# Another fixed order for an attention and expert kernel: 64-row matmul steps in longer runs

## The chip, the core and the metric

The kernel runs on one core of a Trainium2 chip. The metric is the device time of one execution in microseconds. Before the change it is 367.17 us, the median of three runs (366.87 to 367.61). A profiled execution spans 365.3 us; the profile's views count from the start of that span. The core's engines are PE (matmuls, with PEld for loading their weights), DVE (vector), ACT (scalar functions), POOL (GpSimd) and SP, which here only issues transfers. Each engine works through its own instructions in the order in which the program gives them, and waits where it needs another engine's result or a buffer that is still in use.

## What is computed

A linear attention with an exponential feature map, for 8 x 8 heads of 576 tokens and 64 dimensions, and then a two-layer network with an ELU between, for all 4608 tokens:

```python
def phi(x):
    proj = np.einsum('bhsd,df->bhsf', x, w_phi)               # 64 -> 128 features
    proj = proj - np.max(np.abs(proj), axis=-1, keepdims=True)
    return np.concatenate([np.exp(proj), np.exp(-proj)], axis=-1)
q_p, k_p = (phi(q), phi(k))
kv = np.einsum('bhsf,bhsd->bhfd', k_p, v)
z = np.sum(k_p, axis=2)
num = np.einsum('bhsf,bhfd->bhsd', q_p, kv)
den = np.einsum('bhsf,bhf->bhs', q_p, z)[..., None] + 1e-06
x = (num / den)                                               # then heads side by side: 4608 x 512
h = x @ w_in                                                  # 512 -> 2048
g = np.where(h > 0.0, h, np.exp(np.minimum(h, 0.0)) - 1.0)
out = g @ w_out                                               # 2048 -> 512
```

## The kernel before

The 64 heads are worked on in 16 groups of four, and the 4608 tokens of the network in 9 chunks of 512. The program is a list of small steps, each a Python function that emits a few instructions. A string fixes their order: one letter for each step, a star for a variant on another engine or with another layout, and a digit for the first PSUM bank that a PE step writes. The n-th occurrence of a letter is the n-th piece of that kind of work. There are 8 banks; steps A, M, S, U and W take two neighbouring ones, the others one.

```python
ORDER = """
eacdbeefgj7kfA0gj7BekBA2A4fCBj7hl6Bkl1hmBmA6gCBM0BCj3DBkENA4Dl3BEOmBP2l1EQCS2m*CFA0FTM6ECU4DTUNE
...                                     # 30 lines in all
"""
    STEPS = dict(
        ...
        e=(load, ...k...), f=(load, ...q...), g=(load, ...v...),       # POOL issues the loads
        h=(load_w_in, PAIR), i=(load_w_out, [()]),
        j=(t_pe, ...), k=(t_copy, ...), l=(t_pe, ...), m=(t_copy, ...), # k and q of groups 0-3, transposed on PE
        n=(t_dma, [("k", n) for n in range(PT, NG)]),                   # groups 4-15: transposed by DMA, issued by SP
        o=(t_dma, [("q", n) for n in range(PT, NG)]),
        A=(k_mm, ...), B=(k_exp, ...), C=(k_max, ...),                  # k's projection, two exponentials, maximum
        D=(v_exp, ...), E=(v_scale, ...), F=(v_ones, ...),              # v scaled by exp(-max), on POOL
        M=(m_mm, ...), N=(m_max, ...), O=(m_split, ...), P=(m_pe, ...), Q=(m_copy, ...),   # q's maximum
        S=(q_mm, ...), T=(q_exp, ...),                                  # q's projection, exponentials
        U=(kv_mm, ...), V=(kv_copy, ...),                               # kv and z
        W=(x_mm, ...), X=(x_div, ...), x=(x_join, ...), R=(x_rec, ...), y=(x_scale, ...),  # num, den, division
        Y=(x_pe, ...), Z=(x_copy, ...), z=(x_dma, ...),                 # the result transposed
        p=(h_mm, chunk_parts), q=(h_exp, chunk_parts), r=(h_min, chunk_parts), s=(h_elu, chunk_parts),
        t=(o_mm, ...), u=(o_copy, o_tiles), v=(o_store, o_tiles),
    )
    for letter, star, bank in re.findall(r"([A-Za-z])(\*?)(\d?)", "".join(ORDER.split())):
        ...
        fn(*next(args), **how)
```

The steps that the prediction speaks of. The head dimension is 64, so k's and q's projections contract over 64 rows only, and two heads sit above each other in a tile; kv contracts over 64 tokens. These matmuls use half of PE's rows each ("64*128" in the profile); all other steps use the whole array ("128*128").

```python
def k_mm(n, c, bank=None, other=False):                      # A: 6 matmuls, 64 rows
    ...
    for i3 in range(3):
        for par in range(2):
            rows = slice(par * D, (par + 1) * D)
            nc.tensor.matmul(pj[:, par, i3, :], st["kT", n][rows, 3 * c + i3, :], w_sb[rows, :],
                             start=True, stop=True)

def k_exp(n, c, sg):                                         # B, twice on each A's banks: ACT
    nc.scalar.activation(EK[...], st["pk", n, c], ACT.Exp, scale=1.0 - 2.0 * sg)

def k_max(n, c):                                             # C, on the same banks: DVE
    nc.vector.tensor_reduce(mk[...], st["pk", n, c], axis=AX.X, op=ALU.max, apply_absolute_value=True)

def kv_mm(n, pr, bank=None):                                 # U: 36 matmuls, 64 rows
    ...
                    rows = slice(hi * D, (hi + 1) * D)
                    nc.tensor.matmul(kv[:, hi, pr, sg, :], EK[rows, sg, pr * NS + s, :],
                                     vs[rows, sg, pr * NS + s, :], start=(s == 0), stop=(s == NS - 1))

def t_dma(name, n):                                          # n, o: from group 6 on q goes in two halves
    nat = st[name, n // 2][:, 2 * (n % 2):2 * (n % 2) + 2]
    out_t = get((name + "T", n), new_t(name))                # tpool has bufs=2: two kT, two qT
    if name == "q" and n >= JOINED:
        ...
        for hi in range(2):
            nc.sync.dma_start_transpose(out=out_t[:, hi], in_=nat[hi * D:(hi + 1) * D]...)
        return
    ...

def h_mm(ch, jt, h0, h1, bank=None):                         # p: 4 matmuls of 512 columns (chunk 0: 256)
    ...
def h_exp(ch, jt, h0, h1): nc.scalar.activation(e_sb, st["ph", ch, jt, h0], ACT.Exp)      # q: ACT
def h_min(ch, jt, h0, h1): nc.gpsimd.tensor_scalar(e_sb, e_sb, 1.0, 0.0, ...)            # r: POOL
def h_elu(ch, jt, h0, h1): nc.vector.scalar_tensor_tensor(gT[:, jt, h0:h1], e, -1.0, ph, ...)  # s: DVE

def o_mm(ch, tt, part, bank=None):                           # t: 4 matmuls of 512 columns
    ...
```

M works like A on q (the maximum of q's projection has rows and features the other way round than S), S projects q with 64 rows and 384 columns at a time, and W multiplies with all 128 rows. A bank is free for the next PE step when its readers are done: B, B and C for A; T, T for S; N for M; q, r and s for p; u for the last t of an output tile.

Of the kernel before, what the change touches and what calls it, by code (L numbers as in the profile page):

```python
# [15 lines left out]


ORDER = """
eacdbeefgj7kfA0gj7BekBA2A4fCBj7hl6Bkl1hmBmA6gCBM0BCj3DBkENA4Dl3BEOmBP2l1EQCS2m*CFA0FTM6ECU4DTUNE
BM2EOVDBNFW6EP5M0XM2Q*S4ENTU6FNOj1iP0UQ*kTS2VM0TNW4TY7OXS0j6Tl3kTY2mP5l4Z*W0mQ*Z*S3XA5Tp7j2qkTS0  # L20
rCp2TM3TsNqp7BrA0sj4qCp3Brp2qsl6BkresM4qmp7BrNp3qM0qsrA4Drsp6Esp2qNl7Bp3rqp1O*sqrY0mrCZ*W6FEsp0B
XP2gqp5Drp4qQqsrS6srqM2sFTsEM0NTp5rNqp7rS2qsM0sTrY6ENU4TsA0O*A2BUZp7VBp6qP5CBt4rsBS0p7TCtqQ*rW2T
sp5DnXqW0qrtrXfp6ES2qsA0stBnrFsTp7Eu*t6TCp5qp4rDzqp3sqrp2Brszp7sqp5qrqS0rstrTsoFsEqp4Tp7rqzS2sA0
rTtEsCToU4qA2BUrzstV*CBW4up7XW0qBt6rXzDBM4FtNzM0M2sA4NvBp7tNqBzrA0sM2O*BCftBENP7t5uQCEDS2M6TtNFe
TS0M6ETtNTEU2S0A6UTCop4VtqTp3rzBsW0qnp4Xrp2qszW0rqu*O*p3DXvBEp5qsvrp7qrszp6rqsFsA0rqM2np4NBEp5qC
rzP3p2rQ*sqp3srqsDp7rqsfp6sqrBp5rsqEsM0qA2p4NBrt7BrsqFS0CgtTsrTS2EM5TNS0toTsTA5U2CTUBS0VvtBW2zTt
6XTW4uzA0DXS2BtETzCtFETtzBA2M4BS0t7oTCtDTNFtEBvM0A4EM2NBtzNeBU0fu*UA2Cp6Bp5Cqut4rDBsEp7qM2V*rp6N
qEDnW0wstwrqxgM2trNW0FnetxEp5vusS0qM2Rp7syTNp6TFrqS2Rp4qsrTrsp5qsTp7rqysW0qS2xp6rTzrTp4sEzsqA0U2
qCroUrsBp7RV*syA5BCW2p4zxDqW0Eqxp3Brp2rBsRqA0S5qCnt7rTgRtsvTrstBEvsDS3M5TytNzTt2yu*BW3EzS5xA0tBF
zTRM3CtyTNFtzBEwM5S0vU3NTUToA5Vt7BuA0CtCzDtBEW2BtfxBA4p6BRyp3CqDEW0u*wp2qxrBp7FqFsrS0M4TEt6NTtrs  # L30
qtRrsM0ysM3p5NEzp7qNp2rzqsW0rqp4nxrp5qevstrsqsrS0uU2RTUy*S6TzVp4TsW0vqp3xTrp5qoRrsA0qS6p2CTrp4Ts
vqsW6qp3rzBrsp5qexBt2rqRS0DA6srotBsytBsyTA3CtETCzW5Dt7FxFBEtBnRM0yA5M3NBztEutNBzEM0wU2CvfUNDS4V*
Et6uW0TvW2xTtxA4M0BntRBW2Nyzp7ECtqt1xFDrup5FsEA2qM6p4NBrp0ECqU6srBUqM2V*tNrA5sS2Bp7swRp4TRCyqp0T
rztqsBtzrqgy*S2u*W5Torp7xDTp1sqS2qRvW5rsTp4rsTp0zyxqW2Fqp7zrsrsA5qvp1gRBxrp4qsBp3rsqyp2Cqrwzt7sq
rsS0EM5sTtnNTrtEDzsS0M3A5TEtCoTt2NFBEA0U3BCURM5Dty*BEVztBNEW3zu*A0S5xBtTt7CTW3RDtxBEA5wM0Bu*FS3y
tNBEtTCp2TFuW0qU3xM5rURM0NV*p7yNp4zqsrS5qA0p3sTroCp2Tqsp7qrW4qrsp6DrsBnp3Rqsp2qrvxBt7rzqsA0S4srB
tsBp6y*TCzp3qRp2qrvwtrsqzsDtrTEsvM0A3M5NBp2ENp1qBru*p0qEsvt7qCFrM5p2rsW3NqtrstFsExA0S5BtyTCt4TRW
2By*txzDA0U5BRS2zUyBtEV*zCtuFDEvW0TS5xt7TEzTtu*ETS0U2TFS4UwTtVW0p6xp3qRTRW0rtqyTp2rxp5qsp4rqRW0r
sqp6sursp3yqsp7qrzxp5rqy*zp4qrssW0rzqt6Rrsp3zxp7qy*W0rsqp2xrp5qstrsqtRrsp4systqzRp7rzst5qtrvsty*
tzt7ztvttt4ttp3p2qp1rqstrqsp3rsp2qt1rqsp0rsp3qtrqsp2rsp0qu*p3rqvstrqsup6rvsp5qp3rqsp2rqsp6rqstrq  # L40
st5rsp3p6qp2rqstrqsp3rsp6qutrqvsp7rsp3qp6rqstrqsup7rvst4qutrvstup7vp6qtrqst5rsp7u*p6qvtrqstrstt7
p6p4qtrqsp3rstqtrsp6t4qutruvstvtt7utvttt6tutvtt7u*tvttuv
"""


# [769 lines left out]
```

## Time and profile before

| | |
|---|---|
| time, median of 3 runs | 367.17 us |
| span of the profiled execution | 365.3 us |
| granted PE clock | 1.00 in every window, 0.96 in the last (340 us to the end) |
| busy: PE, DVE, ACT, POOL | 347.5, 269.6, 251.8, 213.2 us |
| first matmul | at 4.6 us |
| loads of k, q, v, each batch | 576 KB, landing 7.3 to 9.2 us after their issue (medians) |
| loads of w_in (two), w_out | landing 20.4 us after their issue (medians) |
| tiling changes between PE steps | 160 |

The page's second part cuts the span into 40 slices of 9.1 us and gives each engine's busy share in tenths. Its fourth part follows the chain of waits back from the last instruction. Other views are used below: windows (busy time of each engine in chosen stretches), instructions in order of time (start, length, engine, line, operation, output and inputs, how many), and the source view of one line (how often, how long, from issue to landing for transfers). A line such as L693 is that of the printed kernel: L287 is A, L298 B, L305 C, L346 and L361 M, L469 and L481 S, L509 U, L542 and L558 W, L665 p, L676 q, L681 r, L685 s, L693 t. Matmul ends are modelled in the profile and overlap, so the spacing of starts says what a step costs, not the length of its bar.

### The profile page before, as it was taken

To read this page: it belongs to the slowest core of one execution; us is meant where nothing else is said; L and a number is where in the kernel's file an instruction comes from. 1 tells how busy PE (TensorE), PEld (TensorE's weight loads), DVE (VectorE), ACT (ScalarE), POOL (GpSimd) and SP (SyncE) were. 2 spreads that over 40 slices of the span, in tenths; PEclk is the share of its full clock that TensorE was granted. 3 is DMA by queue.
4 is the path that set the end of the run, shared out by engine and by line. 5 is a ranking of instruction groups with operands and counts; after the bars stand their busy time and mean duration, and the time that the engine had idled before them with its cause. 6 is when DMAs were issued, how large, how long until landed. Compare 5 with 4: busy or idle time off the path is not lost.

```text
span 365.3 us, 9809 instructions
## 1 busy us (share of the span) xinstructions
PE 347.5 (95%) x3914; PEld 188.5 (52%) x3914; DVE 269.6 (74%) x476; ACT 251.8 (69%) x479; POOL 213.2 (58%) x323
## 2 busy tenths in 40 slices
PE   3788899999999999999999999999999999999994
PEld 2566676655465454545455445544555444444442
DVE  4899986878876889798978899899858814744300
ACT  4879788877897689877976886888577304554220
POOL 8673848277934988485776597556557404543200
PEclk9999999999999999999999999999999999999999
DMA  7999969599796999866989399053220330214143
GB/s 106 195 213 208 208 100 148 65 166 151 114 144 95 166 171 144 152 89 92 193 162 126 44 173 135 4 110 79 44 48 16 32 75 2 58 29 92 26 99 74
DMA packets 68478, 39.70 MB, mean 109 GB/s; under 512 B 48336, under 2 KB 62800, under 8 KB 68432
## 3 DMA queue, kind: packets, MB, share of 16 engines
q1 hardware_dynamic: 52416, 20.56, 33.1%
q0 software_dynamic: 15856, 18.35, 32.7%
q8 instruction: 30, 0.49, 0.6%
q14 instruction: 16, 0.13, 0.1%
q10 hardware_dynamic: 160, 0.16, 0.1%
HBM read 36.77 MB, written 9.44 MB: 126 GB/s over the span
## 4 chain that ended last, share of the span: by engine, by line
PE 77%; DVE 12%; DMA 7%; issue 1%; POOL 1%; ACT 0%; DVEq 0%; ACTq 0%; POOLq 0%
PE banks L693 32%; PE banks L665 29%; PE banks L509 4%; DMA kT<-kn 3%; DVE mk L305 3%; PE banks L542 3%; PE banks L469 2%; PE banks L287 2%; DVE gT L685 2%; DMA kn<-in_k_dram 2%; DMA qn<-in_q_dram 2%; PE banks L558 2%; DVE mq L388 2%; PE banks L346 2%; DVE xp L575 1%
## 5 line engine op out<-in xcount | busy, mean ns | idle before, releaser
L681 POOL TENSOR_SCALAR e_sb<-e_sb 128x512 f32<-128x512 f32 (+1 forms) x160 | 91.1, 574 | 96.2 <-ACT e_sb L676 93.1
L693 PE MATMUL banks<-w_out_sb,gT 128*128 128x512 bf16 x576 | 138.3, 380 | 0.0
L676 ACT ACTIVATE e_sb<-banks 128x512 f32<-128x512 f32 (+1 forms) x160 | 88.1, 561 | 62.1 <-PE banks L665 57.9
L685 DVE SCALAR_TENSOR_TENSOR gT<-e_sb,banks 128x512 bf16<-128x512 f32 (+1 forms) x160 | 97.0, 626 | 44.9 <-POOL e_sb L681 44.5
L665 PE MATMUL banks<-xT,w_in_sb 128*128 128x512 bf16 (+1 forms) x576 | 123.0, 356 | 1.1 <-DVE gT L685 0.3
L665 PEld LDWEIGHTS <-w_in_sb 128*128 128x128 bf16 x640 | 59.1, 98 | 58.9 <-issue 2.6
L298 ACT ACTIVATE EK<-banks 128x768 bf16<-128x768 f32 x96 | 75.7, 814 | 16.5 <-PE banks L287 14.5
L324 POOL TENSOR_TENSOR vs<-vn,em 128x576 bf16<-128x576 bf16 x64 | 73.6, 1159 | 17.8 <-ACT em L315 17.7
L693 PEld LDWEIGHTS <-gT 128*128 128x128 bf16 x576 | 52.3, 98 | 59.7 <-issue 1.9
L493 ACT ACTIVATE Eq<-banks 128x768 bf16<-128x768 f32 (+2 forms) x96 | 73.5, 813 | 6.9 <-PE banks L481 3.3
L305 DVE TENSOR_REDUCE mk<-banks 128x6 f32<-128x768 f32 x48 | 45.2, 950 | 6.2 <-ACT EK L298 3.9
L374 DVE TENSOR_REDUCE mx<-banks 128x6 f32<-128x768 f32 (+1 forms) x30 | 30.7, 1038 | 4.8 <-PE banks L346 3.8
L608 POOL TENSOR_TENSOR xj<-xs,recj 128x448 bf16<-128x448 f32 (+1 forms) x22 | 20.1, 916 | 13.9 <-DVE recj L603 10.6
L587 DVE TENSOR_TENSOR xs<-banks,e 128x455 f32<-128x455 f32 (+1 forms) x30 | 18.0, 602 | 7.4 <-PE banks L542 5.9
L703 ACT COPY o_sb<-banks 128x512 f32<-128x512 f32 x23 | 13.3, 589 | 14.5 <-PE banks L693 14.5
L509 PE MATMUL banks<-vs,EK 64*128 64x65 bf16 x1152 | 22.9, 192 | 0.2 <-DVE xp L575 0.2
L509 PEld LDWEIGHTS <-EK 64*128 64x128 bf16 x1152 | 20.9, 96 | 2.9 <-issue 1.3
L542 PEld LDWEIGHTS <-Eq 128*128 128x128 bf16 x400 | 16.2, 97 | 7.3 <-issue 1.3
L592 DVE TENSOR_TENSOR xs<-banks,xs 128x455 f32<-128x455 f32 (+1 forms) x30 | 18.3, 610 | 1.1
L287 PE MATMUL banks<-w_sb,kT 64*128 64x128 bf16 x288 | 17.1, 228 | 1.9 <-DVE kT L240 1.1
L542 PE MATMUL banks<-kv_sb,Eq 128*128 128x65 bf16 x400 | 17.2, 193 | 0.5 <-DVE kv_sb L519 0.5
L469 PE MATMUL banks<-qT,w_sb 64*128 64x384 bf16 (+2 forms) x102 | 16.4, 324 | 0.5 <-DVE gT L685 0.2
(66 smaller groups left out, 243.3 us busy)
## 6 DMA issues: line engine op xcount, KB each, us to landing
out_dram<-o_sb SPq DMA_DIRECT2D x71, 128.0 KB, 2.4
kn<-in_k_dram POOLq DMA_DIRECT2D x7, 576.0 KB, 9.2
qn<-in_q_dram POOLq DMA_DIRECT2D x7, 576.0 KB, 7.3
vn<-in_v_dram POOLq DMA_DIRECT2D x7, 576.0 KB, 8.6
w_in_sb<-in_moe_w_in_dram POOLq DMA_DIRECT2D x2, 1024.0 KB, 20.4
w_out_sb<-in_moe_w_out_dram POOLq DMA_DIRECT2D x1, 2048.0 KB, 20.4
qn<-in_q_dram POOLq DMA_DIRECT2D x2, 288.0 KB, 7.4
vn<-in_v_dram POOLq DMA_DIRECT2D x2, 288.0 KB, 8.1
```

The source lines that it names most:

```text
L298: nc.scalar.activation(EK[:, sg, 6 * c:6 * c + 6, :].rearrange("p (i r) f -> p r i f", r=2), st["pk", n, c], ACT.Exp, scale=1.0 - 2.0 * sg,)
L305: nc.vector.tensor_reduce(mk[:, 6 * c:6 * c + 6].rearrange("p (i r) -> p r i", r=2), st["pk", n, c], axis=AX.X, op=ALU.max, apply_absolute ...
L324: nc.gpsimd.tensor_tensor(get(("vs", n), new_vs)[:, sg, r, 0:D], st["v", n // 2][:, 2 * (n % 2) + pr], st["em", n][:, sg, r].unsqueeze(2). ...
L374: nc.vector.tensor_reduce(mq.rearrange("p (v r) -> p r v", r=2)[:, :, v0:v1], st["pm", n, c][:, :, 0:v1 - v0, :], axis=AX.X, op=ALU.max, a ...
L493: nc.scalar.activation(Eq[:, sg, :, :, p0 * D:p1 * D].rearrange("p h r x -> p r h x"), st["pq", n, c][:, :, 0:(p1 - p0) * P].rearrange("p ...
L509: nc.tensor.matmul(kv[:, hi, pr, sg, :], EK[rows, sg, pr * NS + s, :], vs[rows, sg, pr * NS + s, :], start=(s == 0), stop=(s == NS - 1),)
L542: nc.tensor.matmul(pn[:, sg, v - v0, :], Eq[:, sg, hi, par, i0 * D:(i0 + 2) * D], kv_sb[:, hi, pr, sg, :], start=True, stop=True,)
L665: nc.tensor.matmul(ph, w_in_sb[:, ct, jt * P:(jt + 1) * P], xT_of(ch)[:, ct, h0:h1], start=(ct == 0), stop=(ct == N_CT - 1),)
L676: nc.scalar.activation(e_sb, st["ph", ch, jt, h0], ACT.Exp)
L681: nc.gpsimd.tensor_scalar(e_sb, e_sb, 1.0, 0.0, op0=ALU.min, op1=ALU.max)
L685: nc.vector.scalar_tensor_tensor(gT[:, jt, h0:h1], st["e", ch, jt, h0], -1.0, st["ph", ch, jt, h0], op0=ALU.add, op1=ALU.max,)
L693: nc.tensor.matmul(po, st["gT", ch][:, jt, tt * P:(tt + 1) * P], w_out_sb[:, jt, :], start=(jt == 0), stop=(jt == N_JT - 1),)
```

## The change

Only the order string is replaced. The steps are the same ones, 1797 of them, 550 on PE, with the same stars; what differs is their order on each engine's queue and the banks that PE steps write. The new string lets steps with 64-row matmuls stand together in longer runs, so that PE goes from 64-row to 128-row tiling or back 128 times and not 160. The place of a letter in the string orders it only against steps on the same engine; against other engines it is ordered by the data and buffers that they share.

```diff
@@ -16,30 +16,30 @@
 ORDER = """
-eacdbeefgj7kfA0gj7BekBA2A4fCBj7hl6Bkl1hmBmA6gCBM0BCj3DBkENA4Dl3BEOmBP2l1EQCS2m*CFA0FTM6ECU4DTUNE
-BM2EOVDBNFW6EP5M0XM2Q*S4ENTU6FNOj1iP0UQ*kTS2VM0TNW4TY7OXS0j6Tl3kTY2mP5l4Z*W0mQ*Z*S3XA5Tp7j2qkTS0
-rCp2TM3TsNqp7BrA0sj4qCp3Brp2qsl6BkresM4qmp7BrNp3qM0qsrA4Drsp6Esp2qNl7Bp3rqp1O*sqrY0mrCZ*W6FEsp0B
-XP2gqp5Drp4qQqsrS6srqM2sFTsEM0NTp5rNqp7rS2qsM0sTrY6ENU4TsA0O*A2BUZp7VBp6qP5CBt4rsBS0p7TCtqQ*rW2T
-sp5DnXqW0qrtrXfp6ES2qsA0stBnrFsTp7Eu*t6TCp5qp4rDzqp3sqrp2Brszp7sqp5qrqS0rstrTsoFsEqp4Tp7rqzS2sA0
-rTtEsCToU4qA2BUrzstV*CBW4up7XW0qBt6rXzDBM4FtNzM0M2sA4NvBp7tNqBzrA0sM2O*BCftBENP7t5uQCEDS2M6TtNFe
-TS0M6ETtNTEU2S0A6UTCop4VtqTp3rzBsW0qnp4Xrp2qszW0rqu*O*p3DXvBEp5qsvrp7qrszp6rqsFsA0rqM2np4NBEp5qC
-rzP3p2rQ*sqp3srqsDp7rqsfp6sqrBp5rsqEsM0qA2p4NBrt7BrsqFS0CgtTsrTS2EM5TNS0toTsTA5U2CTUBS0VvtBW2zTt
-6XTW4uzA0DXS2BtETzCtFETtzBA2M4BS0t7oTCtDTNFtEBvM0A4EM2NBtzNeBU0fu*UA2Cp6Bp5Cqut4rDBsEp7qM2V*rp6N
[... the other 21 lines of the old order are cut; the printed kernel has them ...]
+eeacdj2j5kbA0kA3BBBA6CCDBBej1j5kkA1BBBCCfgl0ml3mA4M6A2BBCDDNOfl0ml1m*gCP4M6NBBM0QS2efTTM4FEEhOFE
+EFENNU6UVM0P4Q*OP5Q*DS6M2NNW0XS4Tj3j2TTTj7kA0BBkkA2BCECEhEU4FUS0l7l6VW4mmTTgY1BZ*W6XXiOP0Q*DY5Z*
+S2TTM0NM4Np6qrp7qrFessS2TTl1mp0qA5BBCM3Np7qrp2qp1qrrp6sssrsY4p0p5p2p3qqqO*qrsrsrsrsW6XZ*p1p2p0A4
+qrsqrqrsDFqrBp6qssj3P1QY7BECZkp2S0S4rsqrsTTTl3mM6M0TS2TM4NNNEU6TEEUVA0CA2CBBBp4p5p6W0XzqqO*rsDEr
+sfBqrst7tW1Xttu*P0p6p4qrsqrp3qp5p7p2p6qDrrssqrqQ*ssrqp1qrrp3p7qssqrrsp2qssrsS5S0EEfETTTt3tp2tp7T
+FS0qrsqrTtusTU4FUV*gnA2BBA6BBCCDFeEt0W4tW2ozXXtM6NM4NtuM2NO*A6BBt1nA4BCCBDtzzoM2P7QtS4TNM6Nvtu*
+M2NEEEFfS6TTTU4S0UTTzzA2VzCp6W4Xzovp1p7qDrsqqBBrsW4XO*rsp0qrsp6qA2BCp1p5p4qBp7p3P0qqErsqrsDqQ*nn
+A1rrrFsssBBM5Np4p0p7rsCqErqqrsrp5p6qqrsssM3NS0TzzzTt2p5rsqS0S3oTTTTM6NtrsttS4uM6NgFEEgvvTTU0UVS2
+TTA6BBCDEEt4W0XW2XzzzztA0BBA5CCBBttu*t7S2ToDTA0CBBM5tttM2NNwDA4CBBeFnfeU0EEFUM2Np6V*W4p0W1p3xEEq
[... the other 21 lines of the new order are cut ...]
-p6p4qtrqsp3rstqtrsp6t4qutruvstvtt7utvttt6tutvtt7u*tvttuv
+sp0p7p3p5vruvqqruvssrsqqrsrt1ttstut2tttut5tttt1tttvu*vvuv
 """
```

Of the new order, line 3 holds the first p (`Np6q`), and line 8 the last q projection of group 5 and the first maximum projection of group 7 (`S3oTTTTM6NtrsttS4uM6`).

More of the change, by code (lines that the diff above doesn't have):

```diff
@@ L24 @@
-rTtEsCToU4qA2BUrzstV*CBW4up7XW0qBt6rXzDBM4FtNzM0M2sA4NvBp7tNqBzrA0sM2O*BCftBENP7t5uQCEDS2M6TtNFe
-TS0M6ETtNTEU2S0A6UTCop4VtqTp3rzBsW0qnp4Xrp2qszW0rqu*O*p3DXvBEp5qsvrp7qrszp6rqsFsA0rqM2np4NBEp5qC
-rzP3p2rQ*sqp3srqsDp7rqsfp6sqrBp5rsqEsM0qA2p4NBrt7BrsqFS0CgtTsrTS2EM5TNS0toTsTA5U2CTUBS0VvtBW2zTt
-6XTW4uzA0DXS2BtETzCtFETtzBA2M4BS0t7oTCtDTNFtEBvM0A4EM2NBtzNeBU0fu*UA2Cp6Bp5Cqut4rDBsEp7qM2V*rp6N
-qEDnW0wstwrqxgM2trNW0FnetxEp5vusS0qM2Rp7syTNp6TFrqS2Rp4qsrTrsp5qsTp7rqysW0qS2xp6rTzrTp4sEzsqA0U2
-qCroUrsBp7RV*syA5BCW2p4zxDqW0Eqxp3Brp2rBsRqA0S5qCnt7rTgRtsvTrstBEvsDS3M5TytNzTt2yu*BW3EzS5xA0tBF
@@ L30 @@
[L30 to L41, printed above, removed]
@@ new lines @@
+FS0qrsqrTtusTU4FUV*gnA2BBA6BBCCDFeEt0W4tW2ozXXtM6NM4NtuM2NO*A6BBt1nA4BCCBDtzzoM2P7QtS4TNM6Nvtu*
+M2NEEEFfS6TTTU4S0UTTzzA2VzCp6W4Xzovp1p7qDrsqqBBrsW4XO*rsp0qrsp6qA2BCp1p5p4qBp7p3P0qqErsqrsDqQ*nn
+A1rrrFsssBBM5Np4p0p7rsCqErqqrsrp5p6qqrsssM3NS0TzzzTt2p5rsqS0S3oTTTTM6NtrsttS4uM6NgFEEgvvTTU0UVS2
+TTA6BBCDEEt4W0XW2XzzzztA0BBA5CCBBttu*t7S2ToDTA0CBBM5tttM2NNwDA4CBBeFnfeU0EEFUM2Np6V*W4p0W1p3xEEq
+DuqxrsrsEp4p5p1p0qqrrRssqqqrt3FFrrsRssS4TTS6TTtW1yyxRtp0EvneqrM6M4S1oTTvzzNNwwtuyp7qrssp6qrA0A3B
+CCBp5p2p7U0UgqrssBBqrV*A3CBvnvzzsp6qqrrW0xp5t2BssW3xqrsDDS0TTp7qRFERtS0TTrsEM3A5BCBttNyW0xt7tS5T
@@ new lines @@
+TA3BBCDM0Nttu*uM5NEyEU0FUVA6BBERyCDEA4CEES2TBTBt0tW6xttW1W5zzRu*vzzvzxRyxop4qFrsp3p1p2p5p0wqqrsr
+FqrqqM3ssNrsS6TTt1tM6NA4M2NCRynzy*rsBBvttuzzDp3S4TqoU6UVS1TTTp0qrsW6W4xxp3p2p1qp4p7p6rsqqqFrErrs
+srssp0p5qqA1znrsrRsqqEfrrBBCDEyRyS3TTt7sstttS3oM0NM5Nt2tTTwvuvA0BA3CW6xttBBBA6BFCCEezDFEU0UV*M3N
+t5BW0REuDyEEFA3BBCxS6zzzTTtttuW0S6TTRxRM3Nt2tA0CS5ovTTBBtW3yxtu*vvp5qryRy*M6M3NNsU0UV*p2wwW0xRp7
+p5p6p0qrsqp1qDrrqqrgsqfW2ssxp4qp7p6qrrssrrS2A0RqryysssTTp5p4W2xBBCp6qqqp7qrrssrp2qrrp1qsssrsS4TT
+FDFt0tnnA6CBBS4TTM2Nzzzzozzttt7A5BA1BBBRy*zCM3NttS3TTM5EEEEDgEu*CDEENtu*U0UVS5TTA3CBBt2W0xtRW5xt
@@ new lines @@
+tuA3BBM5NCM0p7p2p6qrp4qqqNRrrsS0TTDwssrsp3qp7p6yyrqrqrsW0p4qt2trsssEp7tqxFFA0CU5M3UNRBBtvu*S0V*T
+TW5rW3xy*xp2qp0wqsRFrsp1p5p6rsqqqrrrp7qrssssp2qrsnoA0CA3Ct5BtBBBtDtvuA6BCM1NW3zyxt5ttDDBS1S3M6NT
+TTTtt0EEEFEM1NU6UV*S3TTtEEFFEW6W1ttvzzu*Ry*ERyxxU5UVS3S1TTwTTvuzzt7tW5W3tRRzzzp2p1p0qqqzyyzzxRxv
+vvW4y*rsxrsp3qtp5p4qqp2rsqrsp0p3p1rrrqRRy*sqsu*W4xt6p7p5qsqrsqtrrp2sqzzyvzzRy*zrrssp0p3p4rqrssqs
+rsqrstp7tut5tttp3qrqp2qrrp0p1sssqqrsp4up7p3p0p2qqp6rrrsssqrqqqrrrsssp5qsrsp7t3tttqrut6p3qrp5p0tt
+tqrqrvut1tsssszp2qp7qttt3vuttp0tt4trsrqrvvvu*p5p6sp3ttt2p1tttqqrrqsqrrsssp5p7p3qrssqrqp1p6qqsrsr
```

## The prediction

> **What bounds the kernel now.** I read the slices of the page first, then the chain that ended last, then the windows, then the instructions in order of time.
>
> ```profile
> PE 347.5 (95%) x3914; PEld 188.5 (52%) x3914; DVE 269.6 (74%) x476; ACT 251.8 (69%) x479; POOL 213.2 (58%) x323
> PE   3788899999999999999999999999999999999994
> DVE  4899986878876889798978899899858814744300
> PE 77%; DVE 12%; DMA 7%; issue 1%; POOL 1%; ACT 0%; DVEq 0%; ACTq 0%; POOLq 0%
> 0.00:10.00 10.00, 3.41 (x32) 2.04 (x32) 4.47 (x10) 4.79 (x7) 8.52 (x17) 1.00 0.77 109
> 30.00:40.00 10.00, 8.98 (x114) 7.02 (x113) 9.92 (x21) 8.99 (x22) 5.61 (x12) 1.00 1.23 208
> 60.00:80.00 20.00, 20.00 (x336) 12.04 (x334) 14.98 (x28) 16.66 (x33) 12.44 (x21) 1.00 0.76 117
> ```
>
> A window row gives length, then the busy time of PE, PEld, DVE, ACT, POOL. Up to about 45 us PE has gaps and DVE is the full engine (9.92 of 10 us from 30 to 40); after that PE is busy in every slice until the last store. So two stretches with two bounds: DVE and the loads at the start, PE afterwards. A time saved on PE counts fully only in the second.
>
> Busy does not mean useful, so I split PE's time further. The spacing from one step's first matmul to the next step's shows what a step really costs:
>
> ```profile
> 149.85 0.34 PE L346 MATMUL banks<-w_sb,qT 64*128 64x128 bf16 x6
> 150.02 0.33 PE L469 MATMUL banks<-qT,w_sb 64*128 64x384 bf16 x2
> ...
> 152.57 0.34 PE L287 MATMUL banks<-w_sb,kT 64*128 64x128 bf16 x6
> 152.84 1.90 PE L693 MATMUL banks<-w_out_sb,gT 128*128 128x512 bf16 x8
> 154.58 0.60 PE L542 MATMUL banks<-kv_sb,Eq 128*128 128x65 bf16 x14
> 155.02 1.03 PE L693 MATMUL banks<-w_out_sb,gT 128*128 128x512 bf16 x4
> 155.98 0.34 PE L287 MATMUL banks<-w_sb,kT 64*128 64x128 bf16 x6
> ```
>
> The first column is the start. Six 64-row matmuls followed by another 64-row step take 150.02 - 149.85 = 0.17 us; the same six followed by a 128-row step take 152.84 - 152.57 = 0.27. Eight 512-column matmuls followed by a 128-row step take 1.74 (0.87 for four); four followed by a 64-row step take 155.98 - 155.02 = 0.96. Each change of tiling, in either direction, costs about 0.10 us. Over all steps of this trace the medians are 0.863 without and 0.959 with a change for four 512-column matmuls, 0.178 and 0.274 for six 64-row ones: **0.096 us a change**.
>
> With such undisturbed spacings for every kind of step, PE's time is: steps 321.8, 160 changes x 0.096 = 15.4, waits 19.0, before the first matmul 4.6, after the last 4.6; together 365.4, the span but for rounding. Of the 19.0 of waits 15.4 lie before 60 us. After 60 us there are only 3.6 in 300 us, so in that stretch the changes are paid in full.
>
> **What the Trainium skill says.** "TensorEngine Tiling (Array Packing)", section Key Properties: changing the tiling mode, not just the tile, drains TensorE. It gives no figure; this trace agrees and gives 0.096 us. "TensorE: Matmul & The Clock Gate", section Back-to-back issue gap: columns / 2.4 + 2.5 ns, which is 216 ns for 512 columns; the trace has 863 / 4 = 216, so PE already runs at that pace and only changes and waits are left to save. "PSUM — Partial Sum Buffer", section on bank collisions: two engines must not use one bank at once, reads included. The trace agrees: DVE's absolute maximum waits for ACT's exponential on the same bank (3.9 us in 6 waits). So a bank with k's projection is held for two exponentials and one maximum, one after another.
>
> **The change, part by part.** Counting letters, both orders have the same 1797 steps, 550 of them on PE, with the same number of starred variants; no engine gets more or less work.
>
> (1) Tiling changes. Walking over the PE letters (A, M, S, U without a star are 64-row, all others 128-row) I count 160 changes before and 128 after: 32 x 0.096 = **3.1 us less on PE**. Not all of it can count: up to the 16th input-layer step (p) there were 30 changes and there are now 22. Those 8 lie where PE waits for DVE, so 8 x 0.096 = 0.8 us buys nothing there. Left: **-2.3 us**.
>
> (2) The start. I add up DVE's work (start-to-start: maximum 0.865, 256-column ELU 0.33, division 1.19 us and so on) from the first maximum to a step that frees a bank PE needs, and subtract the PE work that the order puts between. The largest excess is 8.9 us before and 10.2 after: up to there more DVE work stands ahead of the same PE work. Against this, all of k's first two groups now come ahead of q's, which fills DVE while q still loads: in the old run it idled about 1.9 us between 8.9 and 11.2 us. The order of the first 13 loads on POOL's queue is unchanged; w_in's now stand behind scaling steps, but by my reckoning are still issued before the queue reaches them (old landings 26.4 and 31.4 us). I call the start **even, plus or minus 1.5 us**, beyond the 0.8 already taken off.
>
> (3) A transposed tile's buffer. qT has two buffers, so group 7's transposes cannot start until the last q projection of group 5 has read its own. In the old order at least 9.0 us of PE work stood between that and group 7's first use (the maximum projection M). In the new one I find S3 (group 5) M6 t t t S4 M6 (group 7): 0.18 + 3 x 0.863 + 0.17 and two changes = **3.1 us**. Group 8 has 4.7. The source view of the transposes says how long they need:
>
> ```profile
> L254 SPq DMA_TRANSPOSE qT<-qn x20: 1201/1275/2309, 80.2 to 240.4; - x20
> ...
> DMA to landing us min/median/max: 2.9/4.7/6.3
> ```
>
> One head's landing takes 4.7 us from issue and M of group 7 reads only the first head, so it should wait 4.7 - 3.1 = **1.6 us**; if it must wait for both heads, 1.3 more. Group 8 stands behind another transpose on the same queue and should wait about 0.7. Sum **+2.3 us**.
>
> (4) Other banks. For every PE step I compared the PE work since its bank was last filled with what the readers need (two exponentials and a maximum 2.6 us, exponential, minimum and ELU 2.3). Old: 3 places short, by 0.15 us in all. New: 8 places, by 2.1 in all, mostly behind k's projections. Several of them hide behind one another or behind the wait of (3); I take **+0.5**.
>
> (5) Old waits that may not come back. The old steady stretch had single waits of 0.63 (at 225 us), 0.31 (142) and 0.25 (133); the last two follow a late k tile, which the chain of waits shows from 122 to 134 us. The new order has other gaps there; I take **-0.8**.
>
> Sum: -2.3 + 0 + 2.3 + 0.5 - 0.8 = **-0.3 us**, so 366.9 us.
>
> **Rivals.** A: the drains are all that matters and the new order's waits are as small as the old ones. For it: ACT's and DVE's running sums stay within 0.3 us of PE's in both orders nearly everywhere after the start, so the new order seems built with the same care. Then 367.2 - 3.1 = about 364, or 364.9 with the start's 0.8. B: transposes and loads take the place of the drains. For it: the 3.1 us between S of group 5 and M of group 7, the landings of up to 6.3 us, and chunks 1, 3, 4 and 7, whose transposed input has a margin of 0 to 1 us by my sums, against 3 to 6 before. If M waits for both heads in both groups and two chunks start late, +3 to +4 us on mine: about 370. C: the start stays DVE-bound longer. For it the 10.2 against 8.9; then +1.3, about 368. Against a large loss from C: between the 24th and the 32nd input step the new order has 6.8 us of PE work beside only about 4 of DVE, so DVE catches up there.
>
> **Range and chances.** Rival A's 364 and B's 370 are the ends that I can name; a little outside them I put 363.3 to 370.6. A gain of over 2% needs 359.8 us, more than all 32 changes can give together with the steady waits' 3.6; a loss of over 2% needs 374.5, twice what B costs.
>
> **What would show each step.** Four 512-column matmuls at 0.86 and 0.96 us again, and 128 changes: (1). DVE idle between 8 and 12 us gone, and the accumulated PE wait at about 50 us within 1.5 of the old 20: (2). PE idle of 1 to 3 us at L346, released by the DMA of qT, at about 100 to 120 us: (3); if it is absent, the framework's buffers turn faster than I think. Short PE waits for DVE's maximum (L305): (4). I am wrong if steady waits exceed 9 us, if transposes land later because loads now run at the same time, or if late loads of w_in hold up the first p.

## The result and the profile after

The new order takes **411.96 us** (median of 4 runs, 410.98 to 414.07) against 367.02 for the old one beside it (4 runs, 366.81 to 367.61): ratio **1.1224**, 95% interval 1.1175 to 1.1273. The change made the kernel 12% slower.

The profile page of the new order, its busy line, four of its rows of slices and the shares of the chain that ended last:

```profile
PE 354.5 (86%) x3871; PEld 193.7 (47%) x3914; DVE 271.9 (66%) x476; ACT 254.1 (62%) x479; POOL 213.3 (52%) x323
...
PE   3598889839997679888999799889989999999995
...
DVE  5768976535876347768876699797866794623430
...
PEclk9999999967999869999999999999989999999999
...
PE 56%; DVE 13%; ACT 12%; DMA 11%; issue 5%; POOL 1%; SPq 0%; ACTq 0%; DVEq 0%; POOLq 0%
```

The busy times of DVE, ACT and POOL are within 1% of the old ones: the same work, and 45 to 47 us more of idling on each. PE has holes in slice 9 (82 to 93 us) and slices 13 to 15 (124 to 155 us), single tenths missing up to about 310 us, and a lower granted clock in and after the holes. The chain has changed more than any busy time: ACT had 0% of it before and DMA 7%; now ACT and DMA have 12% and 11%, PE 56% instead of 77%.

The windows of the new order (length, then busy time of PE, PEld, DVE, ACT, POOL, then clock, DMA share, GB/s):

```profile
10.00:20.00 10.00, 5.48 (x61) 3.68 (x60) 7.79 (x13) 7.07 (x16) 6.95 (x9) 1.00 1.19 204
20.00:30.00 10.00, 8.91 (x217) 7.58 (x218) 6.57 (x15) 7.43 (x13) 6.42 (x9) 1.00 0.67 115
...
80.00:100.00 20.00, 12.09 (x154) 5.51 (x151) 8.99 (x12) 6.63 (x11) 5.86 (x8) 0.66 1.13 141
```

and the same first two windows of the old order:

```profile
10.00:20.00 10.00, 8.20 (x147) 6.53 (x148) 8.79 (x15) 8.20 (x17) 6.88 (x9) 1.00 1.20 204
20.00:30.00 10.00, 8.20 (x215) 6.85 (x215) 8.69 (x21) 7.53 (x16) 5.45 (x10) 1.00 1.12 210
```

From 10 to 30 us DVE, which I had called the full engine of the start, is busy 14.4 of 20 us and not 17.5: none of the four engines is full over these 20 us. From 80 to 100 us each of the four is idle for 7.9 us or more.

I split PE's time as in the prediction: spacing of step starts, less the undisturbed spacing of such a step and 0.096 us for each change of tiling.

| us on PE | first matmul | steps | changes | waits | tail | span |
|---|---|---|---|---|---|---|
| old order | 4.6 | 321.8 | 15.4 | 19.0 | 4.6 | 365.3 |
| new order | 4.5 | 321.8 | 12.3 | **69.0** | 4.6 | 412.3 |

The drains fell by the 3.1 us that were promised. Everything else that happened is 50.0 us more of waits. Up to the 299th step of the list (53.7 us in the old run, 59.7 in the new) the waits grew from 15.4 to 23.3; the other 42 us came later, about 25 of them between 80 and 160 us.

The waits view names the partners (engine, line, what it waited for: us in total, times, longest). New order:

```profile
DVE mk L305 <- ACT EK L298: 31.2, 22, 3.6
...
ACT EK L298 <- DVE mk L305: 19.6, 13, 3.6
...
PEld L361 <- DMA qT<-qn: 5.5, 1, 5.5
PEld L346 <- DMA qT<-qn: 5.4, 1, 5.4
...
PEld L361 <- DVE qT L240: 3.9, 4, 3.1
```

Old order:

```profile
DVE mk L305 <- ACT EK L298: 3.9, 6, 2.1
...
ACT EK L298 <- DVE mk L305: 1.8, 4, 0.9
```

L305 is k's maximum on DVE (C), L298 are k's exponentials on ACT (B). Both read the same two PSUM banks. The Trainium skill, "PSUM — Partial Sum Buffer", section "PSUM bank collisions raise a hardware error", says that ScalarE and VectorE must not read one bank at once, so the program lets them in one after the other, in the order of the letters. The trace agrees: in the example below the second reader starts 0.09 us after the first has ended. These waits, of DVE and ACT together and not of PE, grew from 5.7 to 50.8 us. The second group are two waits of 5.5 us for a transposed q.

One such meeting, in the instructions in order of time (start, length, engine, line):

```profile
202.08 0.33 PE L287 MATMUL banks<-w_sb,kT 64*128 64x128 bf16 x6
...
202.35 1.82 DVE L374 TENSOR_REDUCE mx<-banks 128x6 f32<-128x768 f32 x2 [0.52 <-PE banks L346]
...
204.09 0.95 DVE L305 TENSOR_REDUCE mk<-banks 128x6 f32<-128x768 f32 x1
...
205.13 1.51 ACT L298 ACTIVATE EK<-banks 128x768 bf16<-128x768 f32 x2 [3.45 <-DVE denj L599]
...
206.70 0.34 PE L469 MATMUL banks<-qT,w_sb 64*128 64x384 bf16 x2 [1.42 <-ACT EK L298]
```

k's projection starts at 202.08. On these banks the maximum comes first, but on DVE's queue it stands behind two maxima of q, which the same run of 64-row steps had just produced. So it starts at 204.09 and ends at 205.04; ACT, which had nothing else at the head of its queue, sits idle for 3.45 us (the trace names the DVE instruction after the maximum as the releaser) and then needs two exponentials; PE wants the bank for q's projection and waits 1.42 us. A reader that is late by 2 us has stopped three engines.

The two long DMA waits have another look. PE, SyncE (which issues transposes) and POOL (which issues loads) of the new order, from 70 to 93 us:

```profile
85.84 0.50 PE L287 MATMUL banks<-w_sb,kT 64*128 64x128 bf16 x6 [2.20 <-DMA kT<-kn]
86.27 1.89 PE L693 MATMUL banks<-w_out_sb,gT 128*128 128x512 bf16 x4
92.78 0.50 PE L361 MATMUL banks<-w_sb,qT 64*128 64x128 bf16 x6 [4.61 <-DMA qT<-qn]
...
72.19 2.55 SPq L259 DMA_TRANSPOSE kT<-kn  x1
...
79.81 6.87 SPq L259 DMA_TRANSPOSE qT<-qn  x1
...
70.19 0.83 POOL L209 DMA_DIRECT2D qn<-in_q_dram  x1
73.15 0.83 POOL L209 DMA_DIRECT2D vn<-in_v_dram  x1
79.20 0.74 POOL L209 DMA_DIRECT2D kn<-in_k_dram  x1
```

Three loads of 576 KB are under way while group 5's k and q are transposed; the two transposes land 13.6 and 12.9 us after their issue, and q's issue alone takes 6.87 us. At 141 us the same happens to group 8: three loads issued between 130.9 and 132.6 us, the transpose issued at 133.6 lands at 146.6. The skill's "DMA: Bandwidth & Descriptors", section "Queues, rings and completion order", says that each DMA engine takes turns among the queues it has work for. No view here shows the turns themselves; what fits them is that in this trace k's and q's transposes land 2.9 to 4.5 us after their issue with no load in flight, 2.9 to 9.6 beside one or two loads, and 12.2 to 13.6 beside three or more. The number in flight is not the whole of it: in the run with the loads moved, below, three gave 6.7 to 7.9.

### The profile page after: what moved, and what is told of

Read it like the earlier page. It is cut to its first block, busy times and chain, and to the rows that moved or that the text cites. A ratio compares the mean times of both kernels' runs of the same rounds, so it can differ in the third digit from the quotient of the medians.

```text
span 412.3 us, 9766 instructions
## 1 busy us (share of the span) xinstructions
PE 354.5 (86%) x3871; PEld 193.7 (47%) x3914; DVE 271.9 (66%) x476; ACT 254.1 (62%) x479; POOL 213.3 (52%) x323
## 4 chain that ended last, share of the span: by engine, by line
PE 56%; DVE 13%; ACT 12%; DMA 11%; issue 5%; POOL 1%; SPq 0%; ACTq 0%; DVEq 0%; POOLq 0%
PE banks L665 24%; PE banks L693 21%; DMA qT<-qn 8%; ACT EK L298 8%; DVE mk L305 4%; DVE gT L685 3%; PE banks L542 3%; ACT Eq L493 2%; PE banks L509 2%; PE banks L469 2%; DMA kT<-kn 2%; ACT e_sb L676 1%; POOL e_sb L681 1%; PE banks L287 1%; PE banks L346 1%
## 5 line engine op out<-in xcount | busy, mean ns | idle before, releaser
L685 DVE SCALAR_TENSOR_TENSOR gT<-e_sb,banks 128x512 bf16<-128x512 f32 (+1 forms) x160 | 95.9, 627 | 39.7 <-POOL e_sb L681 38.7
L665 PE MATMUL banks<-xT,w_in_sb 128*128 128x512 bf16 (+1 forms) x559 | 119.5, 358 | 2.2 <-DVE mk L305 0.9
L298 ACT ACTIVATE EK<-banks 128x768 bf16<-128x768 f32 x96 | 73.2, 820 | 32.0 <-DVE mk L305 19.6
L665 PEld LDWEIGHTS <-w_in_sb 128*128 128x128 bf16 x640 | 60.8, 98 | 60.5 <-issue 3.8
L324 POOL TENSOR_TENSOR vs<-vn,em 128x576 bf16<-128x576 bf16 x64 | 73.1, 1156 | 27.1 <-ACT em L315 17.5
L493 ACT ACTIVATE Eq<-banks 128x768 bf16<-128x768 f32 (+2 forms) x96 | 72.1, 815 | 21.8 <-PE banks L481 10.8
L693 PEld LDWEIGHTS <-gT 128*128 128x128 bf16 x576 | 53.8, 100 | 66.0 <-issue 9.7
L305 DVE TENSOR_REDUCE mk<-banks 128x6 f32<-128x768 f32 x48 | 45.1, 954 | 32.5 <-ACT EK L298 31.2
L703 ACT COPY o_sb<-banks 128x512 f32<-128x512 f32 x23 | 13.5, 586 | 24.3 <-PE banks L693 24.3
L287 PE MATMUL banks<-w_sb,kT 64*128 64x128 bf16 x288 | 16.0, 230 | 6.9 <-DMA kT<-kn 2.2
```

The costliest lines, as they stand in the source:

```text
L298: nc.scalar.activation(EK[:, sg, 6 * c:6 * c + 6, :].rearrange("p (i r) f -> p r i f", r=2), st["pk", n, c], ACT.Exp, scale=1.0 - 2.0 * sg,)
L305: nc.vector.tensor_reduce(mk[:, 6 * c:6 * c + 6].rearrange("p (i r) -> p r i", r=2), st["pk", n, c], axis=AX.X, op=ALU.max, apply_absolute ...
L324: nc.gpsimd.tensor_tensor(get(("vs", n), new_vs)[:, sg, r, 0:D], st["v", n // 2][:, 2 * (n % 2) + pr], st["em", n][:, sg, r].unsqueeze(2). ...
L493: nc.scalar.activation(Eq[:, sg, :, :, p0 * D:p1 * D].rearrange("p h r x -> p r h x"), st["pq", n, c][:, :, 0:(p1 - p0) * P].rearrange("p ...
L665: nc.tensor.matmul(ph, w_in_sb[:, ct, jt * P:(jt + 1) * P], xT_of(ch)[:, ct, h0:h1], start=(ct == 0), stop=(ct == N_CT - 1),)
L685: nc.vector.scalar_tensor_tensor(gT[:, jt, h0:h1], st["e", ch, jt, h0], -1.0, st["ph", ch, jt, h0], op0=ALU.add, op1=ALU.max,)
```

## Experiments

Two theories stood after this. **D**: loads bunch, transposes come late, PE waits and its clock drops. **H**: the handshake of ACT and DVE over k's banks, badly placed in the queues, holds up everything. A rival to H was that the PE order itself, or the shorter hold of a bank, is what counts. All ratios are against the old kernel on the same chip; a point is a hundredth of the ratio, 3.7 us. PE's waits are those of the profiled execution.

| run | changes | ratio (95% interval) | PE waits, us |
|---|---|---|---|
| new order | 128 | 1.1224 (1.1175 to 1.1273) | 69.0 |
| old start, then new | 140 | 1.0801 (1.0739 to 1.0863) | 52.7 |
| new start, then old | 150 | 1.0253 (1.0190 to 1.0315) | 29.4 |
| new, loads moved | 128 | 1.0811 (1.0732 to 1.0889) | 54.0 |
| new, C freed | 128 | 1.0286 (1.0163 to 1.0409) | 39.4 |
| new, loads moved and C freed | 128 | 0.9948 (0.9926 to 0.9970) | 22.0 |
| new, only C's places changed | 128 | 1.0664 (1.0617 to 1.0711) | 48.1 |
| new PE order, other queues rearranged | 128 | 1.0360 (1.0315 to 1.0404) | 33.9 |
| old, C freed | 160 | 0.9980 (0.9960 to 1.0000) | 18.2 |
| old, only C's places changed | 160 | 1.0511 (1.0469 to 1.0553) | 38.1 |
| old, PE steps moved | 140 | 1.0309 (1.0289 to 1.0328) | 31.8 |
| old, PE steps moved, C freed | 140 | 1.0186 (1.0148 to 1.0223) | 28.7 |
| old, ten steps starred | 140 | 0.9992 (0.9966 to 1.0019) | 18.6 |

**Where: the two halves exchanged.** The list of steps is cut once, and every letter goes on with its next piece.

```diff
-ORDER = new
+ORDER = old[:299 steps] + the rest of new          # and the reverse: new[:303] + the rest of old
```

> The old order for its first 299 steps (to 53.7 us), then the new order's remaining steps in their own sequence; 140 tiling changes. The new order lost 7.9 us on PE up to its own 299th step (23.3 us of waits against 15.35) and 42 us afterwards. Theory D (loads and transposes bunch on the DMA engines from 60 us on, and hold up two first maxima of a group by 5.5 us each): the loads of v's batch 2 now stands in the old part, so the first bunch (60 to 80 us) shrinks and the wait for group 5's transposes, with the half clock after it, goes: about 385 us. Theory H (the handshakes of ACT and DVE over one bank hold up the queues everywhere): only the start's 7.9 us come back, about 404 us. If the two parts were just additive: 404.

> The new order for its first 303 steps (to 59.7 us), then the old order's remaining steps; 150 tiling changes. If the start's loss stands by itself: the old time + 7.9 us of waits - 1 us of changes, about 374 us (1.02). Theory D expects more, up to 385, because k, q and v of batches 2 and 3 start late in the new start and meet in the old rest; theory H expects 374 to 376.

Measured: 1.0801 and 1.0253. The new start costs 2.5 points by itself (waits up to 60 us: 22.8 us against 15.4), and in time (1.0253 x 367 = 376 us) that is theory H's number; D allowed up to 385. The old start gives back 4.2 points, 15 us: more than the start's own 8 us, less than theory D's 27. The wait for group 5's transposes was gone, the one for group 8 stayed (6.8 us at L346). So what the start decides reaches into the second stretch through the loads, and 29 us of the loss belong to the rest.

**Theory D alone: nine loads moved, nothing else.**

```diff
 # place of each load in the list, in us of the new run's PE
-q2 57  q3 67  v2 73  k3 74  v3 123  v4 123  k4 140  q5 140  k5 140
+q2 45  v2 51  q3 57  k3 64  v3 101  k4 107  k5 115  v4 150  q5 156
```

> The new order with nine of the load steps moved, all else in the same sequence: q2, v2, q3, k3 from 57 to 74 us up to about 45, 51, 57, 64 us; v3 from 123 to 101, k4 and k5 from 140 to 107 and 115; v4 and q5, which are used late, from 123 and 140 to 150 and 156 us. Theory D: transposes then land 3 to 6 us after issue as in the old run, the waits of 5.5 us at 86 and 141 us and most of the half clock (13.7 us lost) go: 385 to 392 us. Theory H: at most the two waits go, 401 to 405 us.

Measured: 1.0811, 4.1 points or 15 us less. The source view of the transposes of q in the new order and in this run, minimum, median and maximum from issue to landing; first the new order:

```profile
DMA to landing us min/median/max: 2.9/3.1/13.0
```

with the loads moved:

```profile
DMA to landing us min/median/max: 2.9/3.0/7.9
```

No wait of PE for a transposed q is left in the waits view, and the time at half clock fell from 27.3 us to 6.8. DVE's 30.1 us of waiting for ACT are still there. It lies between the two expectations; D is a real cause, and the smaller one.

**Theory H alone: C takes no part in the banks.**

```diff
         nc.vector.tensor_reduce(
             mk[:, 6 * c:6 * c + 6].rearrange("p (i r) -> p r i", r=2),
-            st["pk", n, c], axis=AX.X, op=ALU.max,
+            fixed, axis=AX.X, op=ALU.max,              # a constant tile of the same shape in SBUF
```

> The new order, but the maximum of k's projection (C) reads a constant tile of the same shape in SBUF instead of the PSUM banks; it leaves out k's maximum (v is scaled by a constant), the instruction counts stay. DVE and ACT then no longer wait for each other over these banks, and the banks come free after the two exponentials. Theory H: the 31 us of DVE's waits for ACT's exponential and the 20 us of the reverse go, PE's waits fall by 20 us or more outside the two DMA waits: 380 to 392 us. Theory D: the short waits shrink a little, the DMA waits and the half clock stay: 402 to 410 us.

Measured: 1.0286, 9.4 points or 34 us less. The ratio counts only the two faster of its four runs (376.5 and 382.0 us); over all four the median is 382.95 us, a ratio of 1.036, and the trace is that of the slowest, 384.5 us. Behind the wait for group 8's q PE waited some 4 us up to the end; in the new order it waited some 21 us there. Three long waits stay (the lines are two further down in this kernel):

```profile
PEld L363 <- DMA qT<-qn: 6.8, 1, 6.8
...
PEld L348 <- DMA qT<-qn: 6.0, 1, 6.0
...
PE banks L695 <- issue: 3.7, 1, 3.7
```

The first two are theory D's; for the third the profile names no cause. With them stay 20.5 us at half clock. It is H's number, 380 to 392 us, with D's waits left untouched. The maximum itself takes as long from SBUF as from PSUM (0.943 us on average, 0.954 in the new order), so a faster reduction is not what helped.

**Both at once.**

> The new order with both cures at once: the nine loads moved, and k's maximum (C) reading a constant SBUF tile (which leaves out k's maximum); 128 tiling changes. Alone, the loads gave 412.0 -> 399.1 (-12.9), the freed C -> 383.0 (-29.0). If the bunched DMA and the handshake over k's banks are two causes beside each other and make up the whole loss: 412.0 - 12.9 - 29.0 = 370 us, and a little under 367 + 0.6 if the drains' 3.1 us come through (364 to 371). If they overlap (the same waits cured twice): 378 to 383. If a third cause exists, it shows as waits that stay.

Measured: **0.9948**. The page of this run:

```profile
PE   3799899999899999999999999999999999999994
...
PEclk9999999999899999999999999999999999999999
...
PE 78%; DMA 6%; DVE 5%; POOL 4%; ACT 4%; issue 1%; SPq 0%; ACTq 0%; POOLq 0%; DVEq 0%
```

PE is full from slice 12 on, the chain has nearly the old shares (78% PE, 77% in the old run), waits are 22.0 us. The single gains add up to 13.5 points, both together gave 12.8, which is equal within the intervals. So the two causes lie beside each other and make up the whole loss. That the saved drains show here is not shown: the old order with C freed has 0.9980 by itself (below), the two intervals overlap, and in the account 3.0 us more of waits than in the old run stand against 3.1 us less of drains. It is no version to use, since it leaves out k's maximum.

**Is it the order, or the shorter hold of the bank?** The freed C also lets a bank go one reader earlier. So I left all readers on the banks and moved only letters C, 42 of 48, by some places; and in the old order those of groups 4 to 15 (the expectation below says 33; all 36 change their place), mostly to directly behind their B's.

```diff
 # new order, only C moved (two excerpts)
-A0kA3BBBA6CCDBBej1j5kkA1BBBCCfg     A0BBA5CCBBttu*t7S2ToDTA0CBBM5
+A0kA3BBBCA6CDCBBej1j5kkA1CBBBfg     A0BBA5BBttCu*t7S2ToDTCA0CBBM5
 # old order, only C moved (excerpt)
-tzBA2M4BS0t7oTCtDTNFtEBvM0A4EM2NBtzNeBU0fu*UA2C
+tzBCA2M4BS0t7oTtDTNFtEBCvM0A4EM2NBtzNeBCU0fu*UA2
```

> The new order with 42 of the 48 k_max steps (C) moved in the text by some places and nothing else: same PE steps, banks and 128 changes, same loads, full computation. Each C then stands where it costs least alternation with ACT's exponentials (B) on the same banks, mostly before them or behind other DVE work. Theory H (handshake on one bank makes DVE and ACT wait on each other): about two thirds of the 29 us that the freed C gave come back, 392 to 396 us. Rival H2 (what helped in the freed run was that banks came free sooner, or that DVE's reduction ran from SBUF, and not the order of the two readers): 408 to 412.

> The old order with 33 of the 48 k_max steps (C) of groups 4 to 15 moved in the text, mostly to directly behind the second exponential (B) of the same banks, so that B B C is the order at 27 places (12 before), and nothing else: same PE steps, banks, 160 changes, loads. If the place of C among its neighbours on DVE and behind ACT is enough by itself to make waits like those of the new order, without any change on PE: 378 to 395 us. If it needs PE's longer 64-row runs to do harm: 366 to 370 us.

> Control. The old order, 160 changes, with k's maximum (C) reading the constant SBUF tile as in the freed runs of the new order (leaves out k's maximum). If the 29 us that the freed C gave in the new order were a gain that any order would have (a faster reduction, a shorter hold of the banks), it shows here too: 355 us or less, as far as PE's 15 us of waits at the start allow. Theory H (only an order that places the readers badly pays for the handshake): the old order has 3.9 us of such waits, none on PE's path after 60 us, so 364 to 368 us.

Measured: moving C alone takes the new order to 1.0664 (391.8 us; H expected 392 to 396), 5.6 of the 9.4 points. The two waits of this pair, 31.2 and 19.6 us in the new order, are now

```profile
ACT EK L298 <- DVE mk L305: 11.5, 12, 2.5
...
DVE mk L305 <- ACT EK L298: 8.3, 12, 1.7
```

Moving C alone in the **old** order, with every PE step, bank, load and all 160 changes as they were, makes it 1.0511. Its waits view:

```profile
DVE mk L305 <- ACT EK L298: 17.7, 19, 3.2
ACT em L315 <- DVE mk L305: 15.5, 13, 3.1
```

The first was 3.9 us in 6 waits. The second (ACT's small exponentials, which need the finished maximum) was 2.8 us in 6 waits. And the old order with C freed is 0.9980: it had nothing to gain. So the place of one reader between two queues is enough to lose 5%. In the new order this place alone accounts for 5.6 of the 12.2 points. The 3.8 points between "moved" and "freed" are not separated: a better place for C, or the shorter hold.

**Does the new PE order have to lose?** Here its PE sequence, banks and 128 changes stay, the loads are those moved before, and the steps of ACT, DVE and POOL are moved among the PE steps.

> The new order's PE sequence, banks and 128 tiling changes, every one kept; the nine loads moved as before; and the steps of ACT, DVE and POOL moved among the PE steps so that readers are not held up in their queues. Full computation. If the order of the readers and loads is the whole cause, and the PE sequence itself is harmless: 365 to 371 us. If the PE sequence with its longer 64-row runs itself makes waits that no order of the readers can take away: 375 us or more.

Measured: 1.0360, 379.2 us, waits 33.9 us. I had expected 365 to 371 us; the number is that of the rival, 375 us or more, for which the PE sequence itself makes waits that no order of the readers can take away. It is far better than 1.0811 with the loads alone, and full computation, but 15 us more of waits than in the old run remain: 3.7 us up to 60 us, and after that fourteen places of 0.4 to 1.2 us and smaller ones. One arrangement does not prove the rival: whether an order of readers exists that serves this PE order without loss stays open.

**The purpose alone, twice.** First fewer changes by moving PE steps of the old order by at most six PE places, with the order on all other engines unchanged:

```diff
 # excerpt
-BtETzCtFETtzBA2M4BS0t7oTCtDTNFtEBvM0A4EM2NBtzNeBU0
+BETzCtttFM4ETzBA2BS0ot7TCDTNttFEBM0A4vM2tENBzNeBU0
```

> The old order with some PE steps moved by at most six PE places, so that 140 tiling changes stand where 160 did; the order on ACT, DVE, POOL and SP is the old one to the letter, as are the banks. This is the change's purpose alone. If a change costs 0.096 us in the steady part: 20 x 0.096 = 1.9 us less at most, some 1.5 us when those in the DVE-bound start count nothing: 365.0 to 365.6 us, ratio 0.995 to 0.996. If moved steps meet readers in the wrong order even over such short ways: the same or up to 3 us slower.

> The order of the run with 140 changes by moving PE steps (378.1 us, 31.8 us of waits on PE against 19.0), with k's maximum (C) reading the constant SBUF tile (leaves out k's maximum). Theory H: what a moved PE step upsets is above all the meeting of ACT and DVE over k's banks; freed, the order needs 364 to 367 us, as the old order freed (366.3) less up to 1.9 us of drains. Rival H3: any bank refilled too early makes the wait (input steps p, q's maximum and exponentials as well), and C has little to do with it: 372 to 378 us.

Measured: 1.0309 and, with C freed, 1.0186. The 1.9 us of drains came (13.4 us of changes on PE), and 12.8 us of waits with them, 7.6 before 80 us and 5.2 after. Freeing C gives back only a part; here H is the smaller cause, and H3's number is the one that came: q's maxima, input steps and kv steps wait in this run as they did before C was freed.

The old trace offers a reason, which no run tests by itself. For every PE step between 60 and 260 us that fills a new bank I took its start less the end of the last reader of that bank: 251 fills, median margin **0.52 us**, 123 of them under 0.5 us. And I looked for 64-row runs that could be put ahead of the 128-row steps before them within that margin: after the first 10 us, one of 80. Only 69 of the 251 fills had the 0.86 us that a move ahead of a single 128-row step of four matmuls needs; there was little slack.

Then fewer changes without moving anything: ten 64-row steps that stand alone take the 128-row layout with zero-padded weights.

```diff
-rqS2Rp4   ysW0qS2xp6   syA5BCW2          # excerpts; five S and five A in all
+rqS*2Rp4  ysW0qS*2xp6  syA*5BCW2
```

> The old order, no step moved; ten 64-row steps that stand alone between 128-row steps (five A and five S) take the 128-row layout that the kernel already has for a starred letter (the weights padded with zeros, same result). 140 changes: 20 x 0.096 = 1.9 us of drains less, but each of the ten steps takes about 0.32 us and not 0.175, +1.45 us: -0.45 us in all, 366.7 us, ratio 0.999. If moving steps is what costs (11 us in the run with 140 changes by moving) and the number of changes is harmless, waits stay at 19 us. If fewer changes themselves somehow made the waits, they rise here too.

Measured: 0.9992 (0.9966 to 1.0019), 366.8 us. In the instructions of this run a starred S:

```profile
127.76 0.49 PE L435 MATMUL banks<-qT,w_pad 128*128 128x384 bf16 x2
128.09 2.75 PE L665 MATMUL banks<-xT,w_in_sb 128*128 128x512 bf16 x11
```

0.33 us from start to start, against 0.17 + 2 x 0.096 = 0.36 with its two drains. On PE: changes -1.9, steps +1.5, waits 18.6 against 19.0. Fewer changes do no harm when nothing moves; the gain is as small as the sum says, and too small for the interval. No full computation that I ran beats the old kernel measurably.

## Why the prediction was wrong

It said 366.9 us, 363.3 to 370.6. The result is 45 us above.

- **(1) Changes: right.** 128 of them, 0.096 us each, 3.1 us less on PE: the new trace has 0.863 us for four 512-column matmuls without and 0.959 with a change, as the old one (216 ns for each; the section that the prediction cites for it calls that the gap of a lone matmul and gives 131 ns for a stream, which neither trace shows). In no full computation did they make the kernel measurably faster.
- **(2) The start, "even, plus or minus 1.5": wrong, 7.9 us.** The step that failed is the sum of DVE's work against PE's work. It holds if DVE always has its next input. Now DVE was idle more (6.57 of 10 us busy from 20 to 30): maxima waited for ACT, copies of transposes stood behind those maxima. The three-engine order was reduced to a sum on one engine. With C freed and the loads moved, DVE was busy 8.96 and 9.09 of 10 us there, and the waits up to 60 us were 15.8; with C freed alone they were 14.6. So this loss is that of (4) again, at the start.
- **(3) The buffer of qT: right gap, wrong landing.** Between S of group 5 and M of group 7 there are 3.1 us in the new trace (the step behind S starts at 119.52, M at 122.65), as predicted, but the first head landed in 2.9 us and group 7 waited nothing. Group 8, for which I had 0.7 us, waited 5.5, and group 5, which I had not listed, 5.5. I took 4.7 us, the old median, as if it belonged to the transpose; it belongs to what runs beside it, 2.9 to 13.0 us for q in the new trace. No buffer held up group 5's q; three loads did. I had named this ("if transposes land later because loads now run at the same time") and given it nothing in the sum.
- **(4) Other banks, "+0.5": the largest error.** The step that failed is the hold of a bank. I took a bank of A as held for 2.6 us and one of p for 2.3, little more than the readers' own durations in a row. In the old trace, between 60 and 260 us, the medians from the end of the fill to the last reader's end are 3.3 and 3.1 us, one in ten over 5.9 and 4.4; in the new one A's median is 3.8 and p's 2.7, so it is k's banks that are held longer. The difference is the time for which a reader stands in its engine's queue. And I tested each bank alone, where a late reader stops its whole engine and with it the readers of other banks. With C out of the banks the kernel gained 34 us.
- **(5) Old waits gone, -0.8:** lost in the rest.
- **Rivals.** B (transposes and loads take over) was right in kind, and gave 370 where its part is about 15 us. C was right that the start costs more, but it gave 1.3 us where the waits grew by 7.9, and DVE was emptier there, not fuller. A's 364 was not reached: with both cures, and without k's maximum, the kernel took 365.2 us, and the old order without it 366.3. What failed in A was that "ACT's and DVE's running sums stay within 0.3 us of PE's" was read as care. A running sum says how much work stands ahead, not who stands behind whom in a queue.

The clock was in no step. The Trainium skill, "TensorE: Matmul & The Clock Gate", sections "What's actually happening" and "HAM oscillation — how this bites in real kernels", says that TensorE falls to half clock after an idle window of about 3.4 us. This trace agrees in the lengths, 13.7, 3.4, 6.8 and 3.4 us at half clock, multiples of 3.4. It does not agree in what stands before them: only the third, from 146.0 us, began in a wait that long (5.3 us). The first began at 84.5 us in a wait of 2.2, before that of 5.5, the second at 135.7 after one of 1.8, the fourth at 306.4 after one of 1.0, while one of 2.8 us that ended at 15.1 passed at full clock. So the length of a single wait does not decide it here, and what does stays open. Counting half of PE's busy time inside those stretches, an estimate, it cost about 10 of the 50 us; 3.4 with the loads moved, 1.7 with both cures.

## What to carry to other kernels

When several in-order engines read the same banks, the order of the readers is part of the schedule: before changing the order on one engine, measure on the trace how long each bank is held and how much margin its next fill has, and expect a shift longer than that margin to come back as waits. Here, savings of a tenth of a microsecond for each change of tiling were lost wherever steps moved for them. A transfer's landing time is read together with what else is in flight at its new place, and PE's waits can cost once more in clock.

## What the runs showed that I had not expected

- A kernel with PE busy over 85% can still lose its clock: 27.3 us at half clock in four stretches, one of them behind a wait of 1.0 us.
- A DMA transpose of half a tile of q, which lands in 2.9 us at best, took 13.0 us with three loads of 576 KB issued just before it; a whole tile, 3.2 at best, took 12.9 and 13.6, and the issue of one of them 6.9 us where 1.3 is the least.
- Where one letter (C) stands among the others is worth 5% of this kernel, with all work, banks and the order of PE's steps the same.
